# A parallel sum of a state-space convolution and a gated MLP: layernorm of the first tiles one by one, aggregates on GpSimd, and a power table laid out entry by entry

## The chip, the cores and the metric

One core of one Trainium2 chip runs the kernel. A core has TensorE (PE; its weight loads are listed as PEld), VectorE (DVE), ScalarE (ACT), GpSimd (POOL) and SyncE (SP), which issues most of the DMAs. Each engine works through its own queue in order, and semaphores tie the queues together. The metric is the device time of one execution, in microseconds (us); lower is better. The times of the kernel before are 229.33, 229.68 and 229.98 us, median 229.68.

## The reference

A token sequence of 2048 tokens with 512 features is normalised, and three things are added: the tokens themselves, a state-space convolution of the normalised tokens (each feature has its own kernel of 2048 taps, a sum of 128 complex exponentials), and a gated MLP of the normalised tokens.

```python
xn = _layernorm(x, axis=-1)                       # x: [1, 2048, 512]
# state-space branch
dt = jnp.exp(log_dt)[:, None]
logdA = dt * (A_re + 1j * A_im)                   # [512, 128]
P = jnp.exp(logdA[:, :, None] * l[None, None, :]) # l = 0..2047, rounded to bf16
K = jnp.einsum("dn,dnl,dn->dl", Cc, P, dt * Bc).real
y = irfft(rfft(xn, 4096) * rfft(K, 4096))[:2048] + xn * Dskip
# gated MLP, F = 1792
h = _sigmoid(xn @ w_gate) * (xn @ w_up)
return x + y + h @ w_down
```

## The kernel before

Tokens lie in 16 tiles of 128 (`NT`), features in 4 pieces of 128 (`KT`), the MLP's width in 14 pieces of 128 (`FT`). Everything is one program without loops at run time: the Python code builds a list of some 940 small operations in a `_Plan`, each with an engine and the operations that it needs, and a hand-kept list `ORDER` says in which order they are written out. Each engine's queue is what `ORDER` leaves of it. Two sets, `ON_DVE` and `UEV`, say which copies run on VectorE and which up products pass through ScalarE first; `ON_ACT` names the token tiles whose statistics ScalarE makes. A change of the number of operations shifts all the numbers in these lists.

What matters here, in the order of time:

- **Start.** `load_x` (line 432) loads token tiles through SP's queue; tiles 0 and 1 come in one load, 2 and 3 in another. `keep_warm` (line 522) gives PE filler matmuls on a zeroed buffer, twenty in one operation and three in each of three more. `layernorm` (line 535) makes the statistics of a tile: on VectorE as `bn_stats` and `bn_aggr` (lines 546 and 547) or on ScalarE as two passes with an accumulated output (540, 541). `ln_small` (line 470) turns them into mean and reciprocal deviation: small operations on VectorE for the first four tiles (487 to 499), on GpSimd for the later groups of four (479 to 481), with the square root always on GpSimd (481, 498). Tiles 0 to 3 are normalised on VectorE (559), transposed on PE (570), and copied by ScalarE into `xnT` (575). Later groups are normalised, stored to DRAM and loaded back transposed.
- **MLP.** For each of four groups of 512 tokens, gate products (line 1031) and up products (1055), four matmuls of 512 columns each; ScalarE's sigmoid (1043), a copy of the up product for those in `UEV` (1066), VectorE's product (1070); then the down projection (1099), 14 matmuls a tile.
- **The convolution's kernel.** From the parameters ScalarE and VectorE make the exponential of one step (`f_sin`, `f_w0`) and square it eleven times (lines 671 to 680); `W` holds these twelve levels in bf16. For each of four chunks of 128 features (`c`), two tables of powers are filled: `G`, 16 entries, and `H`, 41 entries (`NH`), each entry a complex number for 128 modes (partitions) and 128 features. An entry of `H` is a copy of a level of `W` (`seeds`), the product of an earlier entry with a level (`powers`, by `cmul`, lines 736 to 742), or the square of an earlier entry (`squares`, lines 789 to 795). PE then multiplies `G` with `H` for each pair of features (`f_k`, line 821), 128 matmuls a chunk, four at a time on quarters of the array, each with 82 columns: 41 entries for two features. Line 841 picks the results apart.
- **The convolution.** Tokens go through PE twice (lines 697 and 892) with a DRAM round trip between, the kernel is transformed (914), VectorE multiplies the two (919, 923), PE transforms back (936), and after another round trip through DRAM line 995 adds the result; `final` (1010) and line 1119 add up the three terms and store them.

The layout of the tables decides what the engines see. Before, `G` and `H` are [64 feature pairs, entries, 2 components, 2 features of the pair]: the numbers of one pair stand together, entry after entry. In line 821 the moving operand takes, for a fixed component and feature, every fourth element, 8 bytes apart.

Of the kernel before, what the change touches and what calls it, by code (L numbers as in the profile page):

```python
# [10 lines left out]
BF = mybir.dt.bfloat16  # L11
# [3 lines left out]
ALU = mybir.AluOpType  # L15
# [162 lines left out]
def _consts():  # L178
# [22 lines left out]
UEV = (0, 7, 8, 10, 11, 13, 14, 21, 23, 24, 26, 27, 28, 29, 30, 31, 32, 33, 34, 35, 36, 37, 38, 39, 40, 41, 42, 44, 45, 47, 48, 49, 50, 52, 54)  # L201
ON_DVE = (94, 95, 96, 97, 107, 108, 109, 120, 121, 180, 182, 184, 226, 271, 274, 320, 513, 837, 843, 845)
ON_ACT = (0, 2)
ORDER = [
    1, 33, 20, 19, 32, 0, 18, 23, 7, 2, 3, 22, 34, 35, 36, 24, 37, 25, 4, 39, 38, 42, 43, 45, 6, 26, 27, 44, 29, 28,
    40, 41, 47, 5, 30, 21, 31, 614, 591, 9, 10, 12, 617, 603, 604, 592, 50, 46, 11, 48, 51, 90, 89, 652, 623, 626, 49,
    632, 87, 88, 102, 605, 53, 618, 627, 101, 166, 92, 593, 633, 628, 642, 629, 653, 91, 55, 103, 634, 631, 93, 100,
    54, 635, 643, 104, 56, 94, 96, 95, 97, 8, 594, 624, 625, 630, 615, 636, 595, 57, 616, 621, 177, 644, 597, 609, 645,
    610, 637, 58, 52, 59, 647, 598, 60, 646, 61, 105, 185, 106, 599, 638, 186, 62, 611, 648, 600, 649, 141, 596, 601,
    63, 64, 650, 14, 98, 99, 659, 639, 640, 660, 612, 613, 108, 651, 107, 65, 602, 657, 67, 619, 620, 15, 606, 142,  # L210
    607, 167, 658, 110, 654, 66, 144, 655, 641, 214, 68, 189, 661, 145, 608, 622, 113, 698, 725, 143, 13, 168, 656, 70,
    146, 147, 700, 726, 701, 69, 116, 699, 115, 190, 662, 664, 670, 71, 178, 169, 114, 118, 176, 187, 72, 149, 73, 74,
    117, 126, 188, 170, 75, 179, 193, 702, 171, 215, 180, 119, 76, 663, 109, 216, 172, 77, 129, 78, 671, 672, 688, 678,
    665, 120, 194, 127, 128, 173, 195, 79, 196, 121, 673, 689, 679, 708, 709, 728, 80, 718, 729, 730, 719, 81, 156,
    723, 724, 159, 731, 197, 683, 738, 693, 684, 703, 720, 694, 704, 82, 174, 182, 175, 148, 721, 157, 713, 685, 739,
    151, 690, 198, 191, 83, 714, 84, 199, 722, 130, 111, 112, 160, 733, 686, 687, 727, 200, 691, 692, 154, 201, 745,
    695, 696, 715, 203, 734, 705, 706, 183, 152, 85, 697, 204, 202, 192, 716, 743, 86, 744, 131, 680, 155, 158, 205,
    184, 206, 717, 710, 711, 181, 132, 134, 746, 123, 207, 209, 223, 707, 217, 208, 747, 218, 712, 133, 153, 219, 740,
    735, 122, 124, 210, 224, 732, 232, 226, 161, 741, 164, 736, 681, 162, 742, 737, 809, 811, 233, 220, 236, 682, 150,
    16, 17, 229, 812, 806, 804, 225, 227, 165, 805, 136, 139, 234, 221, 163, 237, 235, 222, 240, 137, 125, 807, 140,  # L220
    748, 135, 241, 242, 243, 211, 238, 261, 230, 212, 810, 749, 138, 449, 750, 751, 244, 245, 248, 808, 816, 817, 246,
    247, 228, 250, 213, 262, 249, 794, 814, 756, 251, 263, 434, 450, 451, 453, 435, 231, 436, 239, 252, 253, 758, 264,
    813, 265, 266, 815, 759, 757, 254, 256, 271, 274, 279, 280, 818, 267, 374, 358, 764, 255, 257, 283, 766, 795, 767,
    774, 375, 281, 282, 441, 381, 284, 455, 456, 452, 258, 765, 268, 852, 376, 379, 380, 378, 270, 377, 464, 438, 389,
    850, 259, 287, 853, 288, 272, 273, 260, 775, 269, 440, 769, 779, 276, 770, 382, 781, 457, 289, 383, 851, 454, 458,
    784, 771, 471, 384, 385, 290, 465, 386, 459, 768, 437, 285, 785, 277, 780, 460, 466, 387, 291, 782, 786, 789, 442,
    443, 799, 366, 439, 470, 396, 286, 854, 292, 783, 790, 461, 390, 800, 391, 295, 772, 462, 308, 444, 359, 293, 294,
    445, 275, 309, 787, 297, 773, 788, 298, 296, 826, 829, 367, 824, 825, 310, 393, 368, 830, 472, 801, 827, 299, 300,
    802, 278, 473, 828, 803, 467, 469, 468, 791, 796, 776, 360, 361, 301, 303, 419, 392, 463, 426, 821, 311, 312, 674,
    317, 666, 797, 792, 302, 798, 474, 318, 362, 313, 326, 793, 446, 475, 327, 752, 320, 304, 322, 364, 363, 365, 369,  # L230
    330, 319, 777, 447, 420, 819, 912, 388, 831, 778, 328, 421, 820, 832, 397, 427, 862, 855, 331, 370, 760, 822, 823,
    329, 321, 314, 833, 567, 423, 394, 448, 404, 398, 428, 411, 422, 395, 495, 332, 334, 371, 372, 324, 856, 325, 335,
# [85 lines left out]
def kernel(  # L318
# [113 lines left out]
    def load_x(i0, n):  # L432
        ls = [load("SP", xn[:, i0:i0 + n, :], xv[:, i0:i0 + n, :], 128 * n * KB,
                   pkt=1024 * n)]
        for i in range(i0, i0 + n):
            l_x[i] = ls

    l_x = {}
    load_x(0, 2)
    load_x(2, 2)  # L440
    par = at(OFF["G"], [7, D])
    ld, rawn = par[:, 0, :], {nm: par[:, 1 + qi, :] for qi, nm in enumerate(["Are", "Aim", "Bre", "Bim", "Cre", "Cim"])}
# [27 lines left out]
    def ln_small(t0, t1, deps, prio):  # L470
# [12 lines left out]
        if t1 <= LN_ACT:  # L483
# [9 lines left out]
            def fw_():  # L493
                V.tensor_copy(out=q["m_b"], in_=mv[:, s, 0])
                V.tensor_copy(out=q["m_f"], in_=q["m_b"])
# [692 lines left out]
```

## Time and profile before

| | |
|---|---|
| times of three runs | 229.33 to 229.98 us, median 229.68 |
| the profiled execution's own time | 229.47 us |
| its span (first to last instruction) | 227.4 us |
| PE busy | 216.3 us, 95% |
| PEld busy | 110.4 us, 49% |
| VectorE busy | 202.9 us, 89%, 449 instructions |
| ScalarE busy | 177.1 us, 78%, 287 instructions |
| GpSimd busy | 17.4 us, 8%, 42 instructions |
| clock granted to TensorE in the span | full |
| HBM | 25.28 MB read, 12.06 MB written |

Durations in a trace overlap: the next instruction of VectorE starts before the one in front has ended, and a matmul's recorded duration holds its way through the array, so that four matmuls of 512 columns, each of 380 ns, start 0.86 us after the four before. Busy time counts overlapping durations once.

### The profile page before, as it was taken

To read this page: it belongs to the slowest core of one execution; us is meant where nothing else is said; L and a number is where in the kernel's file an instruction comes from. 1 tells how busy PE (TensorE), PEld (TensorE's weight loads), DVE (VectorE), ACT (ScalarE), POOL (GpSimd) and SP (SyncE) were. 2 spreads that over 40 slices of the span, in tenths; PEclk is the share of its full clock that TensorE was granted. 3 is DMA by queue.
4 is the path that set the end of the run, shared out by engine and by line. 5 is a ranking of instruction groups with operands and counts; after the bars stand their busy time and mean duration, and the time that the engine had idled before them with its cause. 6 is when DMAs were issued, how large, how long until landed. Compare 5 with 4: busy or idle time off the path is not lost.

```text
span 227.4 us, 5412 instructions
## 1 busy us (share of the span) xinstructions
PE 216.3 (95%) x2106; PEld 110.4 (49%) x2106; DVE 202.9 (89%) x449; ACT 177.1 (78%) x287; POOL 17.4 (8%) x42
## 2 busy tenths in 40 slices
PE   7988989999999999999999999899999999999991
PEld 2453434444444644446555666444655555544460
DVE  2999999999999999999989997999939999992663
ACT  5699999999999999767899996966488998761000
POOL 1232200040000000002000032000021000000000
PEclk9999999999999999999999999999999999999999
DMA  6997276200762279419584629944968686798944
GB/s 188 345 395 260 94 187 229 95 0 0 231 138 95 93 230 261 132 30 319 120 236 125 159 88 212 294 145 126 250 173 241 117 246 167 234 240 218 249 172 138
DMA packets 44091, 41.36 MB, mean 182 GB/s; under 512 B 8993, under 2 KB 36002, under 8 KB 44066
## 3 DMA queue, kind: packets, MB, share of 16 engines
q1 hardware_dynamic: 42898, 39.12, 57.5%
q0 software_dynamic: 864, 1.57, 4.2%
q10 hardware_dynamic: 304, 0.33, 0.6%
q8 instruction: 16, 0.26, 0.5%
q14 instruction: 9, 0.07, 0.1%
HBM read 25.28 MB, written 12.06 MB: 164 GB/s over the span
## 4 chain that ended last, share of the span: by engine, by line
PE 53%; DVE 31%; ACT 9%; issue 2%; DMA 2%; SPq 1%; POOL 0%; DVEq 0%; ACTq 0%; POOLq 0%
PE bank L1099 14%; PE bank L1055 9%; PE bank L1031 9%; PE pair L914 5%; DVE hT_sb L1070 5%; ACT big L287 4%; PE pair L936 4%; PE bank L525 4%; PE pair L821 4%; DVE big L736 3%; DVE big L737 3%; DVE stats L546 3%; DVE big L680 3%; DVE big L678 3%; DVE big L742 2%
## 5 line engine op out<-in xcount | busy, mean ns | idle before, releaser
L287 ACT ACTIVATE big<-pair 128x1024 bf16<-128x1024 f32 (+2 forms) x75 | 74.1, 1009 | 12.2 <-PE pair L821 4.2
L1055 PE MATMUL bank<-xnT,wu_sb 128*128 128x512 bf16 x224 | 54.5, 380 | 0.9 <-ACT hT_sb L1043 0.6
L1031 PE MATMUL bank<-xnT,wg_sb 128*128 128x512 bf16 (+1 forms) x220 | 51.2, 368 | 1.0 <-ACT hT_sb L1043 1.0
L1099 PE MATMUL bank<-wd_sb,hT_sb 128*128 128x512 bf16 (+1 forms) x238 | 50.6, 367 | 0.0
L1031 PEld LDWEIGHTS <-wg_sb 128*128 128x128 bf16 x236 | 22.3, 98 | 26.6 <-issue 4.6
L1099 PEld LDWEIGHTS <-hT_sb 128*128 128x128 bf16 x238 | 22.4, 98 | 25.2 <-issue 2.2
L1055 PEld LDWEIGHTS <-wu_sb 128*128 128x128 bf16 x224 | 20.8, 98 | 25.8 <-issue 4.0
L1043 ACT ACTIVATE hT_sb<-bank 128x512 bf16<-128x512 f32 x52 | 31.1, 635 | 0.5 <-PE bank L1031 0.5
L736 DVE TENSOR_TENSOR big<-big 128x1024 bf16<-128x1024 bf16 (+4 forms) x40 | 25.8, 645 | 0.1
L737 DVE TENSOR_TENSOR big<-big 128x1024 bf16<-128x1024 bf16 (+4 forms) x40 | 25.8, 644 | 0.0
L1066 ACT ACTIVATE us_sb<-bank 128x512 bf16<-128x512 f32 x35 | 21.5, 627 | 3.4 <-PE bank L1055 1.8
L919 DVE TENSOR_TENSOR big<-big 128x2048 bf16<-128x2048 bf16 x16 | 19.4, 1219 | 2.3 <-DMA big<-big 2.1
L914 PE MATMUL pair<-big 128*128 128x256 bf16 x160 | 19.6, 272 | 0.3 <-ACT big L287 0.3
L789 ACT ACTIVATE sq_sb<-big 128x256 bf16<-128x256 bf16 (+2 forms) x20 | 12.9, 661 | 6.8 <-DVE big L742 4.7
L914 PEld LDWEIGHTS <-big 128*128 128x128 bf16 x160 | 15.6, 98 | 5.1 <-issue 0.7
L741 DVE TENSOR_TENSOR big<-big 128x512 bf16<-128x512 bf16 (+4 forms) x40 | 16.9, 422 | 0.3
L742 DVE TENSOR_TENSOR big<-big 128x512 bf16<-128x512 bf16 (+4 forms) x40 | 16.8, 419 | 0.0
L1070 DVE TENSOR_TENSOR hT_sb<-hT_sb,us_sb 128x512 bf16<-128x512 bf16 x35 | 14.3, 417 | 0.5 <-ACT us_sb L1066 0.4
L1070 DVE TENSOR_TENSOR hT_sb<-hT_sb,bank 128x512 bf16<-128x512 bf16 x21 | 14.1, 680 | 0.3
L665 ACT ACTIVATE big<-big 128x512 bf16<-128x512 f32 x24 | 14.4, 677 | 0.0
L936 PE MATMUL pair<-big 64*64 64x512 bf16 (+1 forms) x256 | 13.1, 327 | 0.9 <-ACT big L287 0.7
L905 DVE COPY big<-big 32x1024 bf16<-32x1024 bf16 x32 | 13.4, 419 | 0.5
(106 smaller groups left out, 230.9 us busy)
## 6 DMA issues: line engine op xcount, KB each, us to landing
big<-c_E SPq DMA_DIRECT2D x16, 320.0 KB, 4.7
z_scr<-big SPq DMA_DIRECT2D x16, 256.0 KB, 2.8
big<-z_scr SPq DMA_DIRECT2D x16, 256.0 KB, 3.9
v_scr<-big SPq DMA_DIRECT2D x16, 256.0 KB, 3.3
big<-in_A_u_dram SPq DMA_DIRECT2D x4, 512.0 KB, 8.6
big<-big SPq DMA_DIRECT2D x32, 64.0 KB, 2.9
big<-v_scr SPq DMA_DIRECT2D x4, 512.0 KB, 5.7
wu_sb<-in_B_w_up_dram SPq DMA_DIRECT2D x2, 896.0 KB, 13.6
```

Of the source, the lines that this page charges most:

```text
L287: nc.scalar.activation(out=get(out), in_=get(in_), func=ACT.Identity)
L736: V.tensor_tensor(out=wide(outp), in0=wide(lo), in1=mre, op=ALU.mult)
L737: V.tensor_tensor(out=wide(tb()), in0=wide(lo), in1=mim, op=ALU.mult)
L742: V.tensor_tensor(out=outp[:, :, :, 1, :], in0=outp[:, :, :, 1, :], in1=tb()[:, :, :, 0, :], op=opi)
L914: T.matmul(two(sk)[:, o:o + DW], es()[:, g, kt, :], kT[p][:, kt, :], start=kt in (0, NKT - 1), stop=kt >= NKT - 2)
L936: T.matmul(two(sv)[o:o + 64, DW * (2 * g + y):2 * DW * (g + 1)], mab[b:b + 64, 2 * u + g, q, :], pq()[b:b + 64, q, ch] if y else pp()[b:b ...
L1031: T.matmul(bank(sl, k % 2)[:, c0:c1], w[:, kt, k * 128:(k + 1) * 128], xnT[:, grp, kt, c0:c1], start=(kt == 0), stop=(kt == KT - 1))
L1043: S.activation(out=hT_sb[:, hs.idx, k % 2, :], in_=bank(sl), func=ACT.Sigmoid)
L1055: T.matmul(bank(sl), wu_sb[:, kt, k * 128:(k + 1) * 128], xnT[:, grp, kt, :], start=(kt == 0), stop=(kt == KT - 1))
L1066: S.activation(out=us_sb[:, us.idx, :], in_=bank(sl), func=ACT.Identity)
L1070: V.tensor_tensor(out=h(), in0=h(), in1=us_sb[:, us.idx, :] if on else bank(sl), op=ALU.mult)
L1099: T.matmul(bank(po)[:, 0:c[1] - c[0]], hT_sb[:, hts[k // 2].idx, k % 2, jj * 128:(jj + 1) * 128], wd_sb[:, k, c[0]:c[1]], start=first and ...
```

## The change

- **Start.** Tiles 0 and 1 have a load each. Tile 0's statistics move from ScalarE to VectorE. Fourteen fillers instead of twenty stand in the first filler operation. Mean and variance of the first four tiles are written in bf16 directly (`mvb`), which saves two copies.
- **Aggregates.** For tiles 4 to 15 the aggregate on VectorE goes; ten small operations on GpSimd combine the two halves' statistics of four tiles at once, ahead of the square root.
- **Power table.** `H` becomes [41 entries, 2 components, 128 features]: an entry is one contiguous row. `powers` uses the new `cmulh`: where the table has room behind the new entries, both products of a complex multiplication come from one instruction, the second half written into the entries that are filled later; copies and squares that fill such entries wait until they are free again. In line 821 the columns of one matmul are now 41 entries, 512 bytes apart, for each of two features.
- **Order.** `ORDER`, `UEV`, `ON_DVE` (20 operations before, 17 after) and `ON_ACT` ((0, 2) before, (2,) after) are new; among other things SP issues the initial loads in another sequence, and the last work on PE is a half-width down projection instead of the sum of a pair of tiles.

```diff
-ON_ACT = (0, 2)
+ON_ACT = (2,)
...
-    load_x(0, 2)
+    load_x(0, 1)
+    load_x(1, 1)
     load_x(2, 2)
...
         def fn():
-            for i in range(t0, t1):
-                if i in ON_ACT:
...
-            P.tensor_copy(out=q["v_b"], in_=mv[:, s, 1])
-            P.tensor_scalar(out=q["ve_b"], in0=q["v_b"], scalar1=EPS, scalar2=None, op0=ALU.add)
+            m0, v0, m1, v1 = (stats[:, s, x] for x in (1, 2, 4, 5))
+            a, d = mv[:, s, 0], mv[:, s, 1]
+            P.tensor_tensor(out=a, in0=m0, in1=m1, op=ALU.add)
+            P.tensor_scalar(out=mvb[:, s, 0], in0=a, scalar1=0.5, scalar2=None, op0=ALU.mult)
+            P.tensor_tensor(out=d, in0=m0, in1=m1, op=ALU.subtract)
+            P.tensor_tensor(out=d, in0=d, in1=d, op=ALU.mult)
+            P.tensor_tensor(out=a, in0=v0, in1=v1, op=ALU.add)
+            P.tensor_scalar(out=a, in0=a, scalar1=2.0 / D, scalar2=None, op0=ALU.mult)
+            P.tensor_scalar(out=d, in0=d, scalar1=0.5, scalar2=None, op0=ALU.mult)
+            P.tensor_tensor(out=a, in0=a, in1=d, op=ALU.add)
+            P.tensor_scalar(out=mvb[:, s, 1], in0=a, scalar1=0.5, scalar2=None, op0=ALU.mult)
+            P.tensor_scalar(out=q["ve_b"], in0=mvb[:, s, 1], scalar1=EPS, scalar2=None, op0=ALU.add)
             P.tensor_tensor(out=q["sd_b"], in0=q["ve_b"], in1=half[:, s], op=ALU.pow)
...
-    warm = [keep_warm(20, -10)]
+    warm = [keep_warm(14, -10)]
...
                 V.bn_stats(out=stats[:, i, :], in_=xn[:, i, :])
-                V.bn_aggr(out=mv[:, i, :], in_=stats[:, i, :])
+                if i < LN_ACT:
+                    V.bn_aggr(out=mvb[:, i, :], in_=stats[:, i, :])
...
+    def cmulh(full, l0, o0, n, m, conj, fused, deps, prio):
+        ne = n * 2 * CW
+        flat = lambda v: v.rearrange("p k c x -> p (k c) x")
+        lo, outp = full[:, l0:l0 + n], full[:, o0:o0 + n]
+        sl = None if fused else _Slot("tg")
+        tb = lambda: full[:, o0 + n:o0 + 2 * n] if fused else at(TMP["tg"][sl.idx], [2048])[:, 0:ne].rearrange("p (k c x) -> p k c x", c=2, x=CW)
+        def f_a():
+            if fused:
+                V.tensor_tensor(out=full[:, o0:o0 + 2 * n].rearrange("p (w k) c x -> p w (k c) x", w=2),
+                                in0=flat(lo).unsqueeze(1).to_broadcast([128, 2, 2 * n, CW]),
+                                in1=m.unsqueeze(2).to_broadcast([128, 2, 2 * n, CW]), op=ALU.mult)
+                return
+            V.tensor_tensor(out=flat(outp), in0=flat(lo), in1=m[:, 0:1, :].to_broadcast([128, 2 * n, CW]), op=ALU.mult)
+            V.tensor_tensor(out=flat(tb()), in0=flat(lo), in1=m[:, 1:2, :].to_broadcast([128, 2 * n, CW]), op=ALU.mult)
+        def f_b():
+            opr, opi = (ALU.add, ALU.subtract) if conj else (ALU.subtract, ALU.add)
+            V.tensor_tensor(out=outp[:, :, 0, :], in0=outp[:, :, 0, :], in1=tb()[:, :, 1, :], op=opr)
+            V.tensor_tensor(out=outp[:, :, 1, :], in0=outp[:, :, 1, :], in1=tb()[:, :, 0, :], op=opi)
...
-        H = at(OFF["H"], [NPR, NH, 2, 2])
+        H = at(OFF["H"], [NH, 2, CW])
...
         powers(2, 1, 1, 1, [1])
-        squares(5, 2, 1, ["2"])
         powers(3, 1, 2, 2, [1, "2"])
+        squares(5, 2, 1, ["2", "3"])
+        seed(6, 2, ["3"])
         powers(12, 1, 4, 3, [1, "2", "3"])
+        seed(16, 8, ["12"])
         squares(9, 3, 3, ["3", "5"])
-        powers(17, 5, 7, 8, [6, 7, 8, "5", "9"])
+        powers(17, 5, 7, 8, [6, 7, 8, "5", "9", "12"])
...
-            def f_k(half_=half_, sl=sl, G=G, H=H):
+            def f_k(half_=half_, sl=sl, G=G, H4=H.rearrange("p k c (r h) -> p k c r h", h=2)):
...
-                            T.matmul(pk[32 * t:32 * t + 32, y % 4, :], G[:, r, :, comp, h], H[:, r, :, comp, h],
+                            T.matmul(pk[32 * t:32 * t + 32, y % 4, :], G[:, r, :, comp, h], H4[:, :, comp, r, h].rearrange("p k r -> p r k"),
                                      start=(comp == 0), stop=(comp == 1), tile_position=(0, 32 * t))
```

## The prediction

> **What bounds it now.** I read first the page's busy shares, then TensorE (PE) in order of time with the idle time ahead of each piece, then the first 13 us and the last 6 us on all engines, and last the groups with their shapes kept apart.
>
> ```profile
> span 227.4 us, 5412 instructions
> PE 216.3 (95%) x2106; PEld 110.4 (49%) x2106; DVE 202.9 (89%) x449; ACT 177.1 (78%) x287; POOL 17.4 (8%) x42
> ```
>
> PE is the limit. Of its 11.1 us of idle time 1.43 lie before its first matmul and 4.6 after its last. From 12.49 us, where the gate products begin, its only stops over 0.15 us are these (start, length, what; in brackets the stop and who ended it):
>
> ```profile
> 12.49 1.02 PE L1031 MATMUL pair<-xnT,wg_sb 128*128 128x512 bf16 x4 [0.82 <-ACT xnT L575]
> ...
> 21.45 1.02 PE L1031 MATMUL bank<-xnT,wg_sb 128*128 128x512 bf16 x4 [1.01 <-ACT hT_sb L1043]
> ...
> 31.80 1.89 PE L1055 MATMUL bank<-xnT,wu_sb 128*128 128x512 bf16 x8 [0.63 <-ACT hT_sb L1043]
> ...
> 35.24 1.02 PE L1055 MATMUL bank<-xnT,wu_sb 128*128 128x512 bf16 x4 [0.23 <-ACT us_sb L1066]
> ...
> 143.60 1.76 PE L936 MATMUL pair<-big 64*64 64x512 bf16 x32 [0.66 <-ACT big L287]
> ```
>
> with three more of 0.28 to 0.34 at 108, 153 and 167 us. So a change gains by starting PE's real work earlier, ending it closer to the end of the span, or closing these 2.8 us; any longer PE work is paid in full. VectorE (DVE), at 89%, has no stop of PE to its name after 12.5 us.
>
> **Part 1, the start.** Time order again:
>
> ```profile
> 3.88 0.69 DVE L546 BATCH_NORM_STATS2 stats<-big 128x6 f32<-128x512 bf16 x1 [3.88 <-DMA big<-in_A_u_dram]
> ...
> 6.46 0.72 POOL L498 TENSOR_TENSOR ln_sd_b<-ln_ve_b,half 128x2 bf16<-128x2 bf16 x1 [4.89 <-DVE ln_m_b L494]
> ...
> 7.70 0.73 DVE L559 TENSOR_SCALAR big<-big,ln_m_f,ln_ri_f 128x512 bf16<-128x512 bf16 x2
> ...
> 11.43 1.01 ACT L575 ACTIVATE xnT<-pair 128x1024 bf16<-128x1024 bf16 x1
> ```
>
> The first load is now half as large: 128 KiB less at the 345 GB/s of the page's second slice is 0.38 us, so statistics begin at 3.5. Two pairs of statistics and aggregate take 0.82 each (3.88 to 4.70): 5.1, variance 0.17: 5.3. GpSimd's square root then lies hidden, because DVE's queue now has tile 3's statistics (0.8) and the small operations of tiles 2 and 3 before the first reciprocal, and these wait for ScalarE's two passes over tile 2: landing 4.7, passes 1.5 (3.88 to 5.36), small operations 0.8 (5.50 to 6.30) give 7.0. Reciprocal and mean 0.15, applying two tiles 0.73: 7.9 instead of 8.43. Transposes 0.65, copy 1.0: first half of xnT at 9.6. The second half: root again 1.07 (6.30 to 7.37), one 0.6 us product that is now ahead, apply 0.73: 9.6; transposes to 10.3; ScalarE has two short operations (0.74 and 0.52) between the copies, so the second copy ends at 11.9. PE's full-width gate products start there instead of at 12.49, and a half-width one (0.44) that needs the first half alone is placed ahead of them: **-1.0 us**. The six fillers dropped gain nothing of their own: transposes then wait for DVE. Fillers now end near 7.4 (11 at 0.43 us, the rest at 0.22), 0.6 us before the transposes; a granted clock lost there would cost at most what the first 4.7 us at half speed cost, 2.3 us, and I price it at nothing.
>
> **Part 2, loads reordered.** The third gate piece and the second up piece move behind tiles 4 to 11. Up to and with the third gate piece 5.28 MB stand in SP's queue. The windows give 265 GB/s in the first 10 us and 376 in the next: 17.0 us, wanted by PE at about 19 (11.9 plus 7.4 of products that need only what is there). The last up piece is at 6.73 MB, when 6.4 are in by 20.0; wanted at about 22.7; 0 to 1 us late. The three early stops (1.87 us) all ended at ScalarE, which loses tile 0's two passes (1.5 us) but still has three table loads and all sigmoids in the same stretch. I keep 1.5 of the 1.87: **-0.4**.
>
> **Part 3, aggregates on GpSimd.** Three groups of four tiles get ten small operations each before the root, at 0.2 to 0.57 us (lines 479, 480, 713): 3 to 5 us later per group. Behind the waiting reciprocal in DVE's queue stand statistics and up products; DVE, with nine products of 0.6 to 0.7 us and four statistics ahead of it after 11.6, gets there at about 20 us; GpSimd, from 15.5 on, is done at 19.5 to 21. The store and transposed load that follow took 7 us of the 22 between the first store (25.5) and PE's first use for the second token group (after 55). Hidden, 0 to 1 us if not. DVE loses twelve aggregates: 0.80 a pair against 0.69 alone, 1.3 us.
>
> **Part 4, the power table.** DVE: 20 of 40 products are joined to their partners, each saving one instruction's fixed part (a 1024-element product starts 0.60 after the one before, 0.53 of it elements): 1.3 us. Contiguous rows save some 20 to 50 ns in each add and square (below): about 2.8. All of it beside PE: **0** on the path. If PE were quicker it would be worth up to 5 us; it isn't.
>
> The reader of the table is line 821's matmul. Its moving operand took 82 columns 8 bytes apart; now neighbouring columns are 512 bytes apart.
>
> ```profile
> 76.85 2.66 PE L821 MATMUL pair<-big 128*32 128x82 bf16 x128
> ```
> ```profile
> 88.67 0.87 PE L841 MATMUL pair<-big,sw 128*32 128x96 bf16 x64
> ```
>
> Both run four at a time (tile positions 0, 32, 64, 96). Line 821: 2.66 less the last one's 0.26, over 31 steps, is 77 ns for four; line 841, whose 96 columns come in runs of 16, (0.87-0.21)/15 = 44 ns. Per column 0.94 against 0.46 ns: a step of 8 bytes already halves the rate. No row has PE reading at 512. The nearest rows are DVE's, on the same memory (mean ns):
>
> ```profile
> L742 DVE TENSOR_TENSOR big<-big 128x1024 bf16<-128x1024 bf16 x4 | 2.7, 685 | 0.0
> L741 DVE TENSOR_TENSOR big<-big 128x1024 bf16<-128x1024 bf16 x4 | 2.7, 684 | 0.0
> ...
> L741 DVE TENSOR_TENSOR big<-big 128x256 bf16<-128x256 bf16 x8 | 2.4, 306 | 0.0
> L742 DVE TENSOR_TENSOR big<-big 128x256 bf16<-128x256 bf16 x8 | 2.4, 306 | 0.0
> L736 DVE TENSOR_TENSOR big<-big 128x256 bf16<-128x256 bf16 x8 | 2.2, 281 | 0.0
> ...
> L741 DVE TENSOR_TENSOR big<-big 128x128 bf16<-128x128 bf16 x8 | 2.2, 269 | 0.0
> ```
>
> Line 736 (419 ns at 512 elements, 685 at 1024) costs 152 ns plus 0.52 an element. Taking 152 off line 741 leaves, per pair of elements, 1.04 ns where pairs stand 8 bytes apart in runs of eight, 1.20 in runs of two, and 1.83 where each stands alone, 128 or 328 bytes from the next. A lone access costs 1.76 times one in a run. Bounds for line 821: no more than now, if PE pays for any unpacked column alike; a gain I exclude, as no row gets cheaper with a wider step; at most double, two columns per 16 bytes becoming one: +77 ns. I take the 1.76 of the nearest rows: 136 ns, +59 for four. There are 512 matmuls, 128 fours: **+7.5 us**, bounds 0 and +9.9. PE has nothing to hide it behind; ScalarE's copies of the result and all products queued behind move by as much, since neither DVE nor ACT then ends PE's waits.
>
> The Trainium skill speaks against this edit: SBUF — State Buffer, Door 1: The DMA port swizzle, says that SBUF has lines of 16 bytes, that at least two accesses to a line are needed for full bandwidth, and that each step to a new line pays. By it line 821 should have been at full rate before, at about 38 ns for four; the trace has 77, and the measurement decides. On the direction page and DVE's rows agree; the page has no price.
>
> **Part 5, the order of the rest.** Changes between matmul shapes on PE go from 72 to 74, each 0.1 (four products take 0.97 before one, 0.86 otherwise): **+0.2**. At the end:
>
> ```profile
> 222.21 0.62 PE L995 MATMUL pair<-big 128*64 128x512 bf16 x4
> 222.32 0.42 DVE L1119 TENSOR_TENSOR big<-bank,big 128x256 bf16<-128x256 f32 x1
> 222.78 0.38 ACTq L419 DMA_DIRECT2D out_dram<-big  x1
> 222.88 1.22 DVE L1010 TENSOR_TENSOR big<-pair,glu_sb 128x1024 bf16<-128x1024 f32 x1
> ```
>
> Before, a 1.22 us add of a whole pair and a 256 KB store (2.0 to landing, 1.3 of closing) follow the last matmul, 4.6 in all. Now the half-width projection is last: 0.05, add 0.42, 64 KB store 1.83, closing 1.3: 3.6. **-1.0**. The three pair adds are 3 x 1.14 of DVE's time beside 4.8 of PE's, so DVE isn't late. For the stops in between (1.6 us) I assume the same sum, +-1.
>
> **Sum.** -1.0 -0.4 +0.2 -1.0 = -2.2; with line 821, +5.3. The profiled execution took 229.47 (its span and 2.1 around it); the median of the runs is 0.2 more: 229.7 + 5.3 = **235.0 us**.
>
> **Rivals.**
> (A) The wide step costs PE nothing: one column per access is what it pays already. For it: 0.94 ns is close to twice 0.46, as if pairing alone were lost. Against: DVE's rows. Then -2.2, 227.5 us, with its own range 226.5 to 228.8. This is the one on the other side; it decides from +17 ns for four on (2.2/128).
> (B) As A, but early stops grow: last weights 1 us late, GpSimd 1 us late with DVE's products behind it. For it: both margins are under 2 us. Against: PE has 7.4 us of gate products before it needs a bank that ScalarE frees. 229.5 to 230.5.
> (C) The joined product doesn't run at two elements a cycle (its operand is spread over two new dimensions), so does not do what it says: 18 entries x 512 elements x 0.52 ns more, 4.8 us a chunk, 19 in all; less the 5.4 saved and some 8 us that DVE stood idle from 10 to 200 us, +6; DVE becomes the bound: 233 to 234 without line 821's price. Against: line 736's operand is spread in the same manner at full rate.
>
> **Chances.** Forecast 0.60, A 0.27, B 0.08, C 0.05. Range 226.8 to 238.5: from A to the doubled step (229.7 -2.2 +9.9 = 237.4, and 1.1 for the stops); the forecast's own is 232.5 to 238.5. Under 0.3% (0.7 us) no change can be told. Faster: A, 0.27; same: half of B, 0.04; slower: 0.69.
>
> **What would show it.** Line 821's 128 matmuls of a chunk take 4.4 us instead of 2.66, and the DVE rows of the table drop below 269 and 306 ns. The first full-width gate matmul starts near 11.9. After the last matmul 3.6 us remain. GpSimd shows 17 to 25 us busy. If line 821 stays at 2.7 us a chunk, the forecast is wrong and A is what is left.

## The result, and the profile after

The changed kernel takes 236.55 us (median of six runs, 235.71 to 236.96) against 229.66 for the kernel before beside it: a ratio of 1.0283, 95% interval 1.0248 to 1.0319. It is slower by 6.9 us. A second set of six runs gave 236.34 (1.0246, 1.0199 to 1.0294). The profiled execution took 236.77 us, 7.30 more than the one of before.

The page of the changed kernel, first lines:

```profile
span 235.0 us, 5382 instructions
...
PE 223.7 (95%) x2100; PEld 115.5 (49%) x2100; DVE 202.7 (86%) x416; ACT 173.9 (74%) x278; POOL 27.6 (12%) x66
```

PE is busy 7.4 us longer although it has six matmuls fewer (the fillers). Its work in order of time shows where; first the matmul that was line 821 and is now line 859 (start, length, what):

```profile
77.09 4.75 PE L859 MATMUL pair<-big 128*32 128x82 bf16 x128 [0.22 <-DVE big L745]
```

A chunk's 128 matmuls take 4.75 us where they took 2.66. From each four to the next it is 142 ns; before it was 77.5, measured in the same way. The other three chunks read 4.75, 4.74 and 4.74.

PE's stops after the start, same view (in brackets the stop and who ended it):

```profile
11.58 1.05 PE L1069 MATMUL bank<-xnT,wg_sb 128*128 128x256 bf16 x8 [0.59 <-DMA wg_sb<-in_B_w_gate_dram]
12.46 1.03 PE L1069 MATMUL pair<-xnT,wg_sb 128*128 128x512 bf16 x4
...
23.93 2.75 PE L1093 MATMUL bank<-xnT,wu_sb 128*128 128x512 bf16 x12 [0.55 <-DVE hT_sb L1108]
...
33.90 1.02 PE L1069 MATMUL bank<-xnT,wg_sb 128*128 128x512 bf16 x4 [0.59 <-ACT hT_sb L1081]
...
39.81 0.39 PE L1093 MATMUL bank<-xnT,wu_sb 128*128 128x512 bf16 x1 [1.14 <-DVE hT_sb L1108]
...
219.55 0.62 PE L1033 MATMUL pair<-big 128*64 128x512 bf16 x4 [0.28 <-DMA big<-v_scr]
...
221.86 1.05 PE L1033 MATMUL pair<-big 128*64 128x512 bf16 x8 [0.83 <-DMA big<-v_scr]
```

By this view two of the three early stops now end at VectorE, which ended none before. A second profiled execution of the same kernel looks different here:

```profile
12.19 1.88 PE L1069 MATMUL bank<-xnT,wg_sb 128*128 128x256 bf16 x8 [0.67 <-DMA wg_sb<-in_B_w_gate_dram]
...
40.28 1.04 PE L1093 MATMUL bank<-xnT,wu_sb 128*128 128x512 bf16 x4 [1.01 <-DMA xnT<-x_scr]
```

Its stops at 23.9 and 33.9 us are missing, the third ends at a transfer, and its first products take 1.88 us instead of 1.05, because the granted clock is 0.50 from 12.2 to 15.6 us. Its span is 235.0 us all the same. What this says of the forecast is told in the account below. The rows of VectorE's table work, shapes kept apart (busy us, mean ns of one):

```profile
L763 DVE TENSOR_TENSOR big<-big 128x3584 bf16<-128x3584 bf16 x4 | 8.1, 2020 | 0.0
...
L772 DVE TENSOR_TENSOR big<-big 128x256 bf16<-128x256 bf16 x4 | 1.1, 284 | 0.0
...
L772 DVE TENSOR_TENSOR big<-big 128x128 bf16<-128x128 bf16 x4 | 0.9, 219 | 0.0
```

The joined product runs at full rate (3584 elements in 2.02 us; with the fixed part of 152 ns of the prediction taken off, 0.52 ns each, as in line 736 before), and the adds fall from 306 to 284 ns and from 269 to 219. The end, all engines:

```profile
228.47 3.23 PE L1137 MATMUL bank<-wd_sb,hT_sb 128*128 128x256 bf16 x28
...
231.74 0.42 DVE L1157 TENSOR_TENSOR big<-bank,big 128x256 bf16<-128x256 f32 x1 [0.68 <-PE bank L1137]
232.19 0.38 ACTq L420 DMA_DIRECT2D out_dram<-big  x1
```

Set against the forecast, for the two profiled executions (stops are the sums of all gaps between PE's records over 60 ns):

| part | forecast | measured | from |
|---|---|---|---|
| start | -1.0 | -0.9 | full-width gate at 12.46 against 12.49, and eight half-width products (0.88) ahead of it |
| stops up to 41 us | -0.4 | +0.7 | 1.88 before, 2.54 after |
| line 821 | +7.5 | +8.2 | from start to start, 512 matmuls: 10.47 before, 18.71 after |
| later stops | 0 | +0.9 | 1.99 before, 2.89 after |
| mode switches and the rest | +0.2 | 0.0 | what is left |
| tail after PE's last matmul | -1.0 | -1.3 | 4.56 before, 3.28 after |
| outside the span | 0 | -0.3 | 2.07 before, 1.79 after |
| sum | +5.3 | +7.3 | |

### The profile page after: what moved, and what is told of

It is laid out like the page before. It is cut to its first block, busy times and chain, and to the rows that moved or that the text cites. A ratio compares the mean times of both kernels' runs of the same rounds, so it can differ in the third digit from the quotient of the medians.

```text
span 235.0 us, 5382 instructions
## 1 busy us (share of the span) xinstructions
PE 223.7 (95%) x2100; PEld 115.5 (49%) x2100; DVE 202.7 (86%) x416; ACT 173.9 (74%) x278; POOL 27.6 (12%) x66
## 4 chain that ended last, share of the span: by engine, by line
PE 62%; DVE 21%; DMA 7%; POOL 3%; issue 2%; SPq 2%; ACT 1%; DVEq 0%; ACTq 0%
PE bank L1137 18%; PE bank L1069 13%; PE bank L1093 10%; PE pair L859 8%; PE pair L952 5%; DVE hT_sb L1108 5%; DVE big L943 4%; DMA big<-in_A_par_dram 3%; DVE big L957 3%; DVE stats L553 3%; PE pair L974 2%; DMA big<-v_scr 2%; SPq L420 2%; DMA v_scr<-big 2%; DVE big L285 2%
## 5 line engine op out<-in xcount | busy, mean ns | idle before, releaser
L287 ACT ACTIVATE big<-pair 128x1024 bf16<-128x1024 f32 (+2 forms) x73 | 70.7, 989 | 14.9 <-PE pair L859 3.9
L763 DVE TENSOR_TENSOR big<-big 128x2048 bf16<-128x2048 bf16 (+3 forms) x20 | 22.3, 1115 | 5.0 <-ACT big L287 4.7
L1104 ACT ACTIVATE us_sb<-bank 128x512 bf16<-128x512 f32 x35 | 20.9, 606 | 3.3 <-DVE hT_sb L1108 1.6
L957 DVE TENSOR_TENSOR big<-big 128x2048 bf16<-128x2048 bf16 x16 | 19.5, 1219 | 0.4
L859 PE MATMUL pair<-big 128*32 128x82 bf16 x512 | 19.0, 320 | 0.2 <-DVE big L745 0.2
L287 ACT ACTIVATE big<-big 128x256 bf16<-128x256 bf16 x34 | 14.3, 433 | 4.7 <-PE pair L859 4.7
L859 PEld LDWEIGHTS <-big 128*32 128x32 bf16 x512 | 16.2, 115 | 2.9 <-DVE big L745 0.7
L943 DVE COPY big<-big 32x1024 bf16<-32x1024 bf16 x32 | 14.4, 451 | 0.6
L553 DVE BATCH_NORM_STATS2 stats<-big 128x6 f32<-128x512 bf16 x15 | 10.0, 684 | 3.6 <-DMA big<-in_A_u_dram 3.6
```

Source lines behind the costliest of these rows:

```text
L287: nc.scalar.activation(out=get(out), in_=get(in_), func=ACT.Identity)
L763: V.tensor_tensor(out=full[:, o0:o0 + 2 * n].rearrange("p (w k) c x -> p w (k c) x", w=2), in0=flat(lo).unsqueeze(1).to_broadcast([128, 2, ...
L859: T.matmul(pk[32 * t:32 * t + 32, y % 4, :], G[:, r, :, comp, h], H4[:, :, comp, r, h].rearrange("p k r -> p r k"), start=(comp == 0), sto ...
L943: V.tensor_copy(out=half_of(xx, b, 1), in_=half_of(xx, b ^ 1, 0))
L957: V.tensor_tensor(out=pp().rearrange("p q h m -> p (q h) m"), in0=xx().rearrange("p q h m -> p (q h) m"), in1=kb()[:, 0:2 * DW].unsqueeze( ...
L1104: S.activation(out=us_sb[:, us.idx, :], in_=bank(sl), func=ACT.Identity)
```

## The experiments

Times are medians in us; the ratio is to the kernel before in the same set of runs. Line numbers move by a few between kernels; the matmul of line 821 is named so throughout.

### Is the wide step the whole loss?

**The changed kernel with the table as before.** Order, start, aggregates and tail of the change stay; with the table its joined products become two instructions each again.

```diff
-        H = at(OFF["H"], [NH, 2, CW])
+        H = at(OFF["H"], [NPR, NH, 2, 2])
...
-                            T.matmul(pk[...], G[:, r, :, comp, h], H4[:, :, comp, r, h].rearrange("p k r -> p r k"),
+                            T.matmul(pk[...], G[:, r, :, comp, h], H[:, r, :, comp, h],
```

> The changed kernel with the table H laid out as before the change (pairs of features first, products in two instructions, scratch as in the changed kernel); order, start, aggregates and tail stay as changed. Theory (the wide step of PE's moving operand is the loss and VectorE's savings are worth nothing): line 821's matmuls of a chunk fall from 4.7 us back to 2.66, the time by 8.2 us, to 228.3 (227.8 to 229.0), with PE's stops before 41 us at 2.5 us as in the changed kernel. Rival (VectorE's savings carry something: three of the changed kernel's early stops of PE end at VectorE): the stops grow and the time is 229.5 to 231. Second rival (the new order is the loss): it stays above 234.

Measured: 227.78, ratio 0.9895 (0.9854 to 0.9937). In order of time:

```profile
12.17 1.77 PE L1069 MATMUL bank<-xnT,wg_sb 128*128 128x256 bf16 x8 [1.67 <-DMA wg_sb<-in_B_w_gate_dram]
...
40.16 1.04 PE L1093 MATMUL bank<-xnT,wu_sb 128*128 128x512 bf16 x4 [0.88 <-DMA xnT<-x_scr]
...
77.45 2.71 PE L859 MATMUL pair<-big 128*32 128x82 bf16 x128 [0.22 <-ACT big L287]
```

Line 821 is back at 2.71 us a chunk, and 8.8 us of the changed kernel's time are gone (236.55 less 227.78; 8.1 to 8.9 by the ratios of the changed kernel's two sets). Line 821 itself, from start to start, gives 7.8 of them. The layout was all of the loss. What remains of the change gains about 1% against the kernel before; the forecast had -2.2 us for it. VectorE's slower rows cost nothing that shows: the two long stops end at transfers, and three later ones at VectorE (0.28, 0.53 and 0.40 us) stand in the changed kernel too, with its faster rows. The early part of this trace is not a clean comparison: the granted clock is 0.50 from 12.3 to 15.7 us, so that the first products take 1.77 us.

**The kernel before with entry rows only** (the same edit the other way, products not joined).

> The kernel before with only the table H laid out entry by entry; products not joined, order and all else as before. Theory: 82 columns 512 bytes apart cost 146 ns for four matmuls instead of 82, 128 fours, +8.2 us: 237.9 (237.3 to 238.6); VectorE's rows of the table get shorter and nothing comes of it on the path. Rival (part of the loss is the order, and the step costs less where VectorE writes the table in other pieces): 233 to 236.

Measured: 235.85, ratio 1.0267 (1.0207 to 1.0326), in the profiled execution +6.6 us, with line 821 at 142 ns for four as in the changed kernel. So the layout alone makes the kernel before slower, but by less than the 8.2 that line 821 lost. Of the 1.6 us between, some 0.45 come from this execution's start and early stops. The rest comes from PE's four late stops of before (0.34 at 108 us, 0.66 at 143, 0.28 at 153, 0.31 at 167): they are gone, and one of 0.49 at 225 us is new. Either VectorE, done sooner with contiguous rows, had removed them, or a slower PE arrived after what it used to wait for.

**The kernel before with entry rows, read at the old rate.** This tells the two apart; the reading of neighbours is explained below.

> The kernel before with the table laid out entry by entry, products not joined, and in line 821 the neighbours of an entry read one after the other, so that PE's rate is that of before and VectorE's rows are contiguous. It tells where 1.6 us of the 8.2 us went that the layout alone should have cost the kernel before. Theory (PE's four late stops at 108, 143, 153 and 167 us, 1.6 us together, vanish because VectorE is done sooner with its contiguous rows): they vanish here too, 228 to 228.6 with line 821 at 71 ns for four. Rival (they vanished only because a slower PE came later to them): they stay, 229.0 to 229.8.

Measured: 229.16, ratio 0.9992 (0.9958 to 1.0025), line 821 at 74 ns. The stops after 100 us:

```profile
108.12 0.53 PE L863 MATMUL pair<-big,sw 128*32 128x96 bf16 x32 [0.33 <-issue]
166.97 0.56 PE L863 MATMUL pair<-big,sw 128*32 128x96 bf16 x33 [1.05 <-issue]
```

Together they are about as long as before (1.4 against 1.6), but they are not the same stops: the two that ended at ScalarE (143 and 153 us) are down to 0.12 and 0.08, and the one at 167 us, for which the trace names no releaser, has grown from 0.31 to 1.05. The time is the rival's (229.16, forecast 229.0 to 229.8), and VectorE's faster rows are worth nothing that these runs can tell. What removed the single stops stays open.

### What sets the price of a step?

**A sweep of steps.** Each half chunk reads its 82 columns in one run with a step of its own.

```diff
-            def f_k(half_=half_, sl=sl, G=G, H4=...):
+            def f_k(half_=half_, sl=sl, G=G, st=2 ** (2 * c + half_)):
+                Hf = at(OFF["H"], [NH * 2 * CW])
...
-                            T.matmul(pk[...], G[:, r, :, comp, h], H4[:, :, comp, r, h].rearrange("p k r -> p r k"),
+                            T.matmul(pk[...], G[:, r, :, comp, h], Hf[:, 32 * t + 4 * R + h:32 * t + 4 * R + h + 81 * st + 1:st],
```

> The changed kernel with line 821's moving operand read in one run of 82 columns at 2, 4, 8, 16, 32, 64, 128 and 256 bytes, one step for each half chunk (64 matmuls); the numbers read are the wrong ones, so the convolution's kernel is wrong. Theory (what counts is how many columns fall into a line of 16 bytes; pairs 8 bytes apart have two, wider steps one): for four matmuls 38 to 45 ns at 2 and 4 bytes, 80 at 8, 146 at 16 and the same at every wider step. Rival (the cost grows with the distance): about 95 at 16 bytes and 146 only at 256. Second rival (any unpacked column costs alike, and what made the changed kernel slower is something else in its operand, the two runs of 41): 80 at every step from 8 bytes on.

Measured: 233.30 in one execution; only its line 821 is of use, as it reads other columns than the sum needs. In order of time; the last three lines hold two steps each:

```profile
76.87 0.80 PE L860 MATMUL pair<-big 128*32 128x82 bf16 x64 [0.22 <-DVE big L745]
78.29 0.88 PE L860 MATMUL pair<-big 128*32 128x82 bf16 x64 [0.62 <-ACT big L287]
102.64 3.89 PE L860 MATMUL pair<-big 128*32 128x82 bf16 x128
136.00 5.11 PE L860 MATMUL pair<-big 128*32 128x82 bf16 x128
162.11 5.00 PE L860 MATMUL pair<-big 128*32 128x82 bf16 x128
```

From the starts of the single records, first of one four to first of the next:

| step, bytes | 2 | 4 | 8 | 16 | 32 | 64 | 128 | 256 | changed kernel, 512 |
|---|---|---|---|---|---|---|---|---|---|
| ns for four | 38 | 42.5 | 78 | 151 | 152 | 156 | 157 | 143.5 | 142 |

The price doubles from 4 to 8 bytes and again from 8 to 16, and then it is flat: distance does not matter, the number of columns per 16 bytes does. One column per 16 bytes costs 151/82 = 1.8 ns for the four matmuls, two cost 78/41 = 1.9 ns together. The first theory held, the two rivals fell. The Trainium skill (SBUF — State Buffer, Door 1: The DMA port swizzle) has lines of 16 bytes and a penalty for every new line; the edge at 16 bytes agrees. It also says that two accesses to a line give full bandwidth; here two give 78 ns, half the rate of the 38 ns at eight, and the measurement decides.

**Neighbours one after the other.** An entry holds the two features of a matmul 4 bytes apart. Read feature by feature each line is visited twice, far apart in time; read entry by entry it is visited once, for both.

```diff
-T.matmul(pk[..., y % 4, :], G[:, r, :, comp, h], H4[:, :, comp, r, h].rearrange("p k r -> p r k"),
+T.matmul(pk[..., y % 4, :].rearrange("p (r k) -> p k r", r=2), G[:, r, :, comp, h], H4[:, :, comp, r, h],
```

> The changed kernel, line 821 alone altered: the 82 columns are taken entry by entry with the two features of an entry (4 bytes apart) one after the other, and the result is written to the same places as before, now 164 bytes apart in turn. Theory (the sweep's cost per line of 16 bytes visited, 0.45 ns for each of four matmuls' lines: 41 lines instead of 82): 76 ns for four as before the change, 2.7 us a chunk, -7.8 us, 228.3 to 229.5, with VectorE's contiguous rows kept. Rival (two columns of one line are not joined when the step alternates, or the scattered writes cost as much): 136 ns or more, 236 to 237.

Measured: 227.01, ratio 0.9882 (0.9809 to 0.9955).

```profile
span 224.9 us, 5355 instructions
```
```profile
76.77 2.64 PE L859 MATMUL pair<-big 128*32 128x82 bf16 x128 [0.22 <-DVE big L745]
```

The layout, VectorE's rows and every address are those of the changed kernel; only the order of reading differs, and 9.5 us are gone (8.4 to 9.2 by the ratios), 74 ns for four instead of 142. Line 821 itself gives 8.4 of them. This one line makes the changed kernel faster than the kernel before.

**Four columns to a line.** The table as pairs, component, entry, feature, so that columns stand 4 bytes apart; products then take four instructions of half the length on VectorE. The aggregates are back on VectorE too, as in the runs of the next part.

```diff
-        H = at(OFF["H"], [NH, 2, CW])
+        H = at(OFF["H"], [NPR, 2, NH, 2])
...
+            for o, q in ((outp, 0), (tb(), 1)):
+                for w in range(2):
+                    V.tensor_tensor(out=o[:, :, w], in0=lo[:, :, w], in1=mb(q).unsqueeze(2).to_broadcast([128, NPR, n, 2]), op=ALU.mult)
```

> The order, start and tail of the changed kernel, aggregates on VectorE, and the table H in a third layout: pairs of features first, then component, entry, feature of the pair, so that line 821's columns are 4 bytes apart, four in a line of 16 bytes. Products take four instructions of half the length. Theory: line 821 takes 43 ns for four as in the sweep, 1.4 us a chunk; against the table as before with aggregates on VectorE (estimated at 227.8 less 1.4) a gain of 4.2 us: 222.2 (221 to 224). Rival (VectorE, some 5 us longer with the shorter instructions, becomes the bound): 224.5 to 228.

Measured: 230.32, ratio 1.0022 (0.9988 to 1.0057).

```profile
PE 211.5 (92%) x2073; PEld 106.1 (46%) x2100; DVE 209.4 (92%) x496; ACT 173.9 (76%) x278; POOL 17.4 (8%) x39
```
```profile
79.75 0.87 PE L864 MATMUL pair<-big 128*32 128x82 bf16 x64 [0.84 <-ACT big L287]
...
105.17 1.80 PE L864 MATMUL pair<-big 128*32 128x82 bf16 x128
```

Line 821 does what the sweep said (43 ns; 1.8 us in the chunk without a stop), but the rival won: VectorE is busy 209.4 us, 5.7 more than in the kernel with both repairs below, and PE stops for ScalarE and VectorE, among them 0.84 us in the middle of line 821. The PE time that was saved came back as waiting. That VectorE's extra instructions are what made ScalarE late fits the sizes; no run took them away alone.

### The other parts

**Aggregates back on VectorE**, in the changed kernel.

```diff
-            P.tensor_tensor(out=a, in0=m0, in1=m1, op=ALU.add)
...
-            P.tensor_scalar(out=mvb[:, s, 1], in0=a, scalar1=0.5, scalar2=None, op0=ALU.mult)
...
-                if i < LN_ACT:
+                if True:
                     V.bn_aggr(out=mvb[:, i, :], in_=stats[:, i, :])
```

> The changed kernel with the aggregates of tiles 4 to 15 back on VectorE, in the place of their statistics, written in bf16; GpSimd keeps the addition of epsilon and the root. Theory (GpSimd's ten operations take 5.7 us beside VectorE's work, VectorE's reciprocal waits 1.8 us for them, and the products behind it make PE stop at 23.9 and 39.8 us): the stops before 41 us fall from 2.5 us to 1.3 to 2.0, the time by 0.5 to 1.2 us, to 235.3 to 236.0. Rival (VectorE is late in this stretch anyway, and 1.3 us of aggregates more make it later): the stops stay or grow, 236.3 to 237.3.

Measured: 235.18, ratio 1.0227 (1.0187 to 1.0267). In its trace the first reciprocal behind GpSimd's root starts at 21.09 us instead of 22.24, and PE's stops at 23.9 us and at the transposed load are gone. The median is 1.2 to 1.4 us under the changed kernel's, but the intervals overlap. **Both repairs together** (this edit and the neighbours' order):

> The changed kernel with both repairs: neighbours of an entry read one after the other in line 821, and the aggregates back on VectorE. Theory (the two gains, 9.5 and 1.4 us, lie in different stretches and add up): 227.0 less 1.4, 225.6 (225.0 to 226.4). Rival (with PE 8 us shorter VectorE is the next bound, and 1.3 us more of it give the second gain back): 226.5 to 227.5.

Measured: 227.32, ratio 0.9901 (0.9873 to 0.9928), against 227.01 without this edit: no gain. The two reciprocals in VectorE's queue say a part of why:

```profile
20.87 0.17 DVE L503 RECIPROCAL ln_ri_f<-ln_sd_b 128x4 f32<-128x4 bf16 x1
...
40.55 0.17 DVE L503 RECIPROCAL ln_ri_f<-ln_sd_b 128x4 f32<-128x4 bf16 x1
```

In the changed kernel they start at 22.24, after a wait of 1.83 us for GpSimd, and at 40.32. VectorE gains 1.4 us at the first and has paid them back, in aggregates, at the second. PE doesn't get all of the 1.4 in between: its stop at 24.0 us is still 0.67 long and now ends at the last piece of the up weights, which landed at 23.99 in this execution and at 22.70 in the changed kernel's. PE reaches line 821 0.43 us sooner than with the aggregates on GpSimd (76.34 against 76.77) and leaves its first chunk 0.09 sooner, after a stop for ScalarE in the middle. GpSimd's aggregates were about neutral here: what they spare VectorE it waits for.

**The changed kernel again**, because the runs with aggregates on VectorE and with products not joined both lacked the two stops near 220 us.

> The changed kernel itself, once more. With aggregates on VectorE it took 235.18 and with products not joined 235.66, both less than its own 236.55; in both profiles the two stops of 1.1 us ahead of line 1033 near 220 us are gone, which neither edit touches. Theory (these stops come and go with the landing of a transfer, and the changed kernel was measured high): 235.2 to 236.0, and neither edit gained anything. Rival (both edits gain what they seem to): 236.3 to 236.9.

Measured: 236.34, ratio 1.0246 (1.0199 to 1.0294), and one stop of 0.63 us there. By the medians the theory fell. But the kernel before took 230.77 beside it, against 229.66 to 230.36 in the other sets, and by the ratios the changed kernel (1.0246 here), the aggregates on VectorE (1.0227) and the products not joined (1.0243) lie within one another's intervals. Whether either edit gained anything is open. Why an edit 200 us earlier should remove these stops is open; they end at the landing of the gathered `v_scr`, and they differ between executions of one kernel (1.11 us and 0.63).

**Products not joined**, in the changed kernel.

```diff
-            if fused:
-                V.tensor_tensor(out=full[:, o0:o0 + 2 * n].rearrange("p (w k) c x -> p w (k c) x", w=2), ...)
-                return
             V.tensor_tensor(out=flat(outp), in0=flat(lo), in1=m[:, 0:1, :].to_broadcast([128, 2 * n, CW]), op=ALU.mult)
             V.tensor_tensor(out=flat(tb()), in0=flat(lo), in1=m[:, 1:2, :].to_broadcast([128, 2 * n, CW]), op=ALU.mult)
```

> The changed kernel with each joined product made by two instructions again, into the same places. Theory (the joined product's saving lies beside PE and is worth nothing): 20 more instructions of VectorE, 1.3 to 2 us of its time, the end within 0.7 us of the changed kernel, 235.8 to 237.2. Rival (VectorE now stops PE, so its time counts): 237.2 to 238.5.

Measured: 235.66, ratio 1.0243 (1.0186 to 1.0300). VectorE is busy 203.4 us instead of 202.7, and the kernel is not slower. The joined product does what it says and is worth nothing on the path.

**The tail as before**: in `ORDER`, the last pair's projection, add and store (operations 754, 755, 756) go behind the half-width down projection.

> The changed kernel with the last pair of tiles' projection, its add of 1.22 us and its 256 KB store written out behind the half-width down projection instead of ahead of it, so that the end is built as before the change. Theory (after PE's last matmul 4.6 us follow instead of 3.3): +1.3 us, 237.5 to 238.3. Rival (the pair's data came late anyway, 0.8 us of PE's stops before line 1033 wait for them, and these go): +0.2 to +0.8.

Measured: 237.63, ratio 1.0328 (1.0261 to 1.0395). After PE's last matmul 4.5 us remain instead of 3.3. The medians agree with +1.3 (1.1 and 1.3 against the changed kernel's two sets), the intervals of the two kernels overlap.

**The second gate piece ahead of tiles 4 to 7** on SyncE's queue, in the kernel with both repairs: `7, 10, 6, 5` becomes `7, 6, 10, 5` in `ORDER`.

> The kernel with both repairs, and on SyncE's queue the second piece of the gate weights (384 KB) issued ahead of the 512 KB load of tiles 4 to 7. Theory (after the start of the changed kernel, PE's first gate product waits not for the normalised tiles but for this piece, which lands at 11.6 us): it lands about 1.7 us sooner, PE's 0.6 us stop goes, -0.4 to -0.7 us against the kernel with both repairs. Rival (tiles 4 to 7 land 1.3 us later, and VectorE's statistics and what stands behind them with them): 0 to +0.6.

Measured: 228.67, ratio 0.9942 (0.9918 to 0.9966), 1.35 us slower than without it.

```profile
10.47 0.60 PE L1058 MATMUL bank<-xnT,wg_sb 128*128 128x256 bf16 x4
...
11.55 0.69 DVE L542 BATCH_NORM_STATS2 stats<-big 128x6 f32<-128x512 bf16 x1 [1.64 <-DMA big<-in_A_u_dram]
...
18.77 1.46 PE L1082 MATMUL bank<-xnT,wu_sb 128*128 128x512 bf16 x6 [1.43 <-ACT hT_sb L1070]
```

PE's first gate product starts 1.1 us sooner, as the theory had it. But VectorE now waits 1.64 us for tiles 4 to 7, and seven microseconds later PE stops for 1.43. In this stretch an earlier PE is given back as soon as VectorE or ScalarE is later; the changed kernel's second execution shows the other side, a PE that was later by up to 2.2 us and cost nothing.

## Why the prediction was right, and where not

- **The line that decides.** Right in mechanism and nearly in size: 142 ns for four against 136 forecast. The prediction left the mechanism open between a price for each 16 bytes that an access opens and one for any unpacked column; the sweep settled it for PE, and rival A (the wide step costs PE nothing) fell. That VectorE's factor (1.76) came so close to PE's (1.83) may be luck: no run shows that VectorE pays by the same 16 bytes.
- **"PE has nothing to hide it behind".** Right for the changed kernel (8.8 us came back when the layout was undone), too strong for the kernel before, where some 1.1 of the 8.2 us were covered by stops that PE had there anyway.
- **Start, -1.0.** In the first profiled execution the size was right, half of the reason wrong. Normalising went as worked out: the first half of `xnT` was there at 9.58 (forecast 9.6), the second at 11.83 (11.9). But the full-width products did not start at 11.9; the second piece of the gate weights landed at 11.53, against 10.50 before the change: the load of tiles 4 to 7 now stands ahead of it, and the eight half-width products that fit before the full-width ones began only then. Part 2 looked at the third gate piece and the last up piece, not at the second gate piece.
- **The clock, priced at nothing.** Right in the first profiled execution, where the granted clock stays at 1.00. In the second, and in the one with the table as before, it reads 0.50 for 3.4 us from 12.2 and 12.3 us on. PE had stood idle 1.60 and 1.67 us shortly before, waiting for VectorE or the gate weights; in the nine other traces of kernels with the new order such waits are at most 1.47 us, and none lost its clock. In the second execution this put PE 1.6 us further back by 23.7 us, inside the 2.3 that the forecast allowed for, and cost nothing in the end: the stops that followed in the first execution were gone, and both spans are 235.0. That fewer fillers are the cause is not shown; no run put them back.
- **Loads and early stops, -0.4, and "hidden" aggregates.** Wrong: +0.7. Two steps failed. The first is that ScalarE alone ends these stops. The one at 23.93 ended at VectorE, whose products stood behind the reciprocal that waited 1.83 us for GpSimd. The forecast had both facts (VectorE there at about 20 us, GpSimd done at 19.5 to 21, products behind the reciprocal) and priced them at 0 to 1; VectorE was there at 20.4, GpSimd done at 22.2. GpSimd's busy time was 27.6 us where 17 to 25 were expected. This is rival B's mechanism, beside the forecast instead of in place of it. The weights' share of it was forecast well as a wait (0 to 1 us late): in two other traces this stop ended at the last up piece (0.67 us with both repairs, 0.80 with the products not joined). The third gate piece landed at 18.97 instead of 17.0, and PE did not wait for it.

  The second step is the room for store and transposed load. "PE's first use for the second token group (after 55)" is a misreading. Already before the change PE started products of that group at 39.56 (its 15th gate product, where a group has 14), 6.6 us after their load had landed at 32.95:

```profile
39.56 1.03 PE L1031 MATMUL bank<-xnT,wg_sb 128*128 128x512 bf16 x4
```

  (The "7 us of the 22" is a slip as well: from 25.5 to 55 are 29.6 us.) In the changed kernel the store and the load were issued here:

```profile
27.65 0.40 SPq L420 DMA_DIRECT2D x_scr<-big  x1
28.09 0.51 SPq L420 DMA_DIRECT2D wd_sb<-in_B_w_down_dram  x1
31.32 5.87 SPq L591 DMA_TRANSPOSE xnT<-x_scr  x1
```

  The store is 2.1 us later than before (25.53). The transposed load lands at 39.77, 8.4 us after its issue instead of 4.5; the load of the down weights now stands ahead of it and was behind it before. That this is what slowed it fits the times, but no run turned the two round. PE's third stop ended at 39.81, when both this load (39.77) and VectorE's product (39.80) were done; the view names the later one. In the second execution, and with neighbours paired, it names the load.
- **Aggregates "hidden", VectorE -1.3.** As it came out: a wash, 227.32 against 227.01 with and without.
- **VectorE's table savings, 0.** Right on the path, too large in VectorE's time: 4.1 us were forecast, and VectorE is busy 204.4 us with the table as before and 202.0 to 202.7 with the changed one, 1.7 to 2.4 less. With the slower layout back (227.78) or the joined products undone (235.66) nothing was lost, and the contiguous rows alone gave the kernel before nothing (0.9992). Rival C, a joined product off its full rate, fell: 2.02 us for 3584 elements.
- **Later stops, 0 +-1.** +0.9 in the first profiled execution. Of the 2.89 us 1.11 end at the transfers near 220 us, which vary (0.63 in the second). But 1.20 end at VectorE, 0.28 at 181, 0.52 at 190 and 0.40 at 207 us, and these stand, within 0.12 us, in every trace of a kernel with the new order, also where the table or the aggregates are as before, and in none with the order of before. So they come with the new order, for which the forecast's "neither DVE nor ACT then ends PE's waits" did not hold. Which moved operation makes them was not tested.
- **Tail, -1.0.** -1.3 in the profile; putting the old order back cost 1.1 to 1.3 on the medians.

The total missed by 1.5 us in the medians and by 2.0 in the profiled executions: 0.7 from line 821's size, 1.1 from the early stops and 0.9 from the late ones, less 0.3 each from the tail and from the time outside the span, with start and mode switches making up the rest. That it came so near is in part that such errors have both signs. One sum of the forecast is off without bearing on it: the stops that it lists come to 3.5 us, not 2.8.

## What to carry to other kernels

Before a table is laid out for the engine that writes it, count for the engine that reads it how many neighbouring elements of one access sequence fall into the same 16 bytes, above all where matmuls run four at a time on parts of the array; the order of reading can repair a layout without moving a byte. Price a saving by the engine that ends the waits there: some two microseconds of VectorE's time were worth nothing, sixty-five nanoseconds of PE's in a line that runs 128 times were worth eight microseconds. When loads are reordered, look for the first consumer of each piece that moved back, not only of the last one, and look it up in the trace. And profile a kernel twice before a stop of half a microsecond is given a cause.

## What the runs showed of the hardware

- GpSimd's small operations take 0.20 to 0.24 us when VectorE works on one input from SBUF or takes one from PSUM, and wait for VectorE's instructions with two inputs from SBUF. The changed kernel in order of time:

```profile
30.54 0.67 DVE L686 SCALAR_TENSOR_TENSOR big<-big 128x512 f32<-128x512 f32 x1
30.61 1.27 POOL L481 TENSOR_TENSOR mv<-stats 128x4 f32<-128x4 f32 x1
31.13 0.69 DVE L688 TENSOR_TENSOR big<-big 128x512 f32<-128x512 f32 x1
...
31.96 0.20 POOL L482 TENSOR_TENSOR mv<-mv 128x4 f32<-128x4 f32 x1
...
33.38 1.38 POOL L487 TENSOR_SCALAR mvb<-mv 128x4 bf16<-128x4 f32 x1
33.39 0.69 DVE L686 SCALAR_TENSOR_TENSOR big<-big 128x512 f32<-128x512 f32 x1
```

  The operation that starts at 30.61 ends at 31.88, with the second of VectorE's two (31.13 to 31.82); the one at 31.96, four columns too, takes 0.20. In the first group, beside a row of such products of VectorE, eight operations took 0.52 to 0.71 each, 5.7 us with the last two of 0.2 that ran while VectorE stood idle. The Trainium skill (SBUF — State Buffer, Terms) has a port pair that the two engines lock for a whole instruction; the trace agrees.
- The matmul with paired neighbours writes its 82 results alternately 164 bytes apart in PSUM; at 74 ns for four it is no slower than the 77.5 with neighbours next to each other.
- Beyond 16 bytes the step costs the same up to 128 bytes (151 to 157 ns), and a little less at 256 and 512 (143.5 and 142).
- The granted clock reads 1.00 in the changed kernel's first profiled execution and 0.50 from 12.2 to 15.6 us in its second; eight half-width products took 1.05 us in the one and 1.88 in the other.
